# Linear attention on one core: the first v from two queues, another order of the first four heads, and v in two groups of eight tiles in every buffer

## The chip, the cores and the metric

The kernel runs on one core of a Trainium2 chip. TensorE (PE) multiplies, with its weight loads shown apart (PEld); VectorE (DVE), ScalarE (ACT) and GpSimd (POOL) do elementwise work; SyncE (SP) issues the DMA transfers, which 16 DMA engines carry out. The metric is the device time of one execution in microseconds, the median of several runs. It holds the profile's span, from the first to the last instruction, and a little around it.

## The reference

Inputs q, k and v and the output are bf16 arrays of 1 x 32 x 2048 x 128: 32 heads, 2048 positions, 128 columns.

```python
phi_q = jnp.where(q > 0, q + 1, jnp.exp(q)) + 1e-6
phi_k = jnp.where(k > 0, k + 1, jnp.exp(k)) + 1e-6
kv = jnp.einsum("bhsd,bhse->bhde", phi_k, v)
z = jnp.einsum("bhsd->bhd", phi_k)
num = jnp.einsum("bhqd,bhde->bhqe", phi_q, kv)
den = jnp.einsum("bhqd,bhd->bhq", phi_q, z)[..., None] + 1e-6
return num / den
```

## The kernel before

A head's 2048 positions lie on 128 partitions, 16 consecutive positions on each, so that a load or a store moves one run of 4,096 bytes per partition, and position tile j is the j-th position of every partition. The feature map is split as phi(x) = min(exp(x), 1) + 1e-6 + max(x, 0). The first part is called emk or emq, the second rk or rq, and most products are made twice, once with each, and added up in PSUM.

The steps of a head, with the names that the profile shows:

- ScalarE makes ek = exp(k) (line 276). VectorE makes emk of it (L282). GpSimd makes rk (L279; for head 1 VectorE does), and for tiles 1 to 5 it adds emk into rk (L287), which spares their second product.
- TensorE forms kv, summed over the 16 tiles, in one PSUM bank (L297 and L236). The sum z is formed beside it, as one more column. In SBUF, v lies between strips of ones (GAP, 32 columns). A tile at the edge of a group takes a column of ones in with its 128 columns of v, so its matmul has 129 columns. For every other tile a second matmul of one column follows with the weights still in place (`mm_held`, L236). The list `GROUPS` gives the number of groups of v in each of the six input buffers: one group of 16 tiles in buffers 0 to 3, two groups of 8 tiles in buffers 4 and 5. Head h uses buffer h mod 6. A load of v (L269) moves one run of 4,096 bytes per partition for one group, two of 2,048 for two.
- ScalarE copies kv to SBUF (kvs, L306), and VectorE adds the two columns of z to it (zs, L308).
- TensorE transposes the 16 tiles of q into xT (tr, L315). ScalarE makes eq = exp (L322) and the second half of rq (L330), VectorE the first half of rq (L326; all of it for heads 0 and 1) and emq (L333).
- TensorE multiplies both parts by kvs (num, L349 and L350), five PSUM banks to a head. VectorE adds 1e-6 to the denominators (den, L371), takes reciprocals (L377) and multiplies (L382, L389). SyncE stores the head (L434; the last one in two pieces of 288 and 224 KB).

`Plan` holds the order. Every step is added with an engine and a key; each engine runs its steps by rising key, in one queue, and waits on semaphores for what it reads or overwrites. A key is the head's number plus an offset of the step; the table `place` (L251) gives other keys to some steps of heads 0 to 3 and of the last head. On TensorE the order is tr(0), kv(0), tr(1), num(0), kv(1), tr(2), kv(2), num(1), tr(3), kv(3), num(2) and so on. SyncE's loads run ahead by up to six heads, as buffers come free; stores have keys that fall further behind from head to head (L438), with ten output buffers. Ahead of the first transposes, 42 matmuls on zeros (L242 to L247) run on TensorE, and GpSimd makes the identity and the ones (L227 to L234).

Of the kernel before, what the change touches and what calls it, by code (L numbers as in the profile page):

```python
# [11 lines left out]
def _ap(base: bass.AP, elem_offset: int, dims):  # L12
    return bass.AP(base.tensor, base.offset + elem_offset, [list(base.ap[0])] + [list(d) for d in dims])
# [131 lines left out]
def bass_standalone__linear_attn_elu__prompt_kernel(  # L145
# [6 lines left out]
    B, H, S, D = q.shape  # L152
    assert D == P and S == 16 * P
    NT = 16
# [3 lines left out]
    NBI = 6  # L158
    NBO = 10
# [3 lines left out]
    HALF = NT * P // 2  # L163
# [2 lines left out]
    ADD = (1, 2, 3, 4, 5)  # L166
    SPLIT = tuple(j for j in range(NT) if j not in ADD)
    GAP = 32
    GROUPS = (1, 1, 1, 1, 2, 2)
    VW = NT * D + 3 * GAP  # L170

    qf = q.rearrange("b h s d -> (b h) s d")
    kf = k.rearrange("b h s d -> (b h) s d")
# [3 lines left out]
    with ExitStack() as es:  # L177
        def sb(name, shape, dt):
            return es.enter_context(nc.sbuf_tensor(name, shape, dt))

        k_sb = sb("k_sb", [P, NBI, NT * D], bf16)
# [22 lines left out]
        def dma_sem(name):  # L204
            return dsems[name]

        for n, c in (("k", NBI), ("q", NBI), ("v", NBI), ("o", NBO + 1)):
            for i in range(c):
                dsems[(n, i)] = es.enter_context(nc.semaphore(f"s_{n}{i}"))

        block = es.enter_context(nc.Block())
        pl = Plan()

        def rows(x, h):
            return x[h].rearrange("(p j) d -> p (j d)", j=NT)

        vfull, ofull = v_sb[:, :, :], o_ps[:, :]
        xfull = xT_ps[:, :].bitcast(fp32)

        def vcol(bi, j):  # L220
            n = NT // GROUPS[bi]
            return GAP * (j // n + 1) + D * j, j % n == 0, j % n == n - 1

        zero_sb = o_sb[:, NBO - 1, 0, :]
# [3 lines left out]
        pl.add("pool", -8, lambda g: g.affine_select(out=ident[:], in_=ident[:], compare_op=ALU.not_equal, fill=1.0,  # L228
                                                     base=0, pattern=[[-1, P]], channel_multiplier=1),
               reads=[("id0",)], writes=[("ident",)])  # L230
        n1 = GROUPS.count(1)
        pl.add("pool", -7, lambda g: g.memset(_ap(vfull, 0, [[VW, n1], [GAP + NT * D, 2], [1, GAP]]), 1.0), writes=[("vones", 1)])
        pl.add("pool", -6.5, lambda g: g.memset(_ap(vfull, n1 * VW, [[VW, NBI - n1], [GAP + NT * D // 2, 3], [1, GAP]]), 1.0),
               writes=[("vones", 2)])  # L234
        def mm_held(pe, out_ap, rhs, stop):
            return pe.add_instruction(mybir.InstMatmult(  # L236
                start_tensor_calc=False, stop_tensor_calc=stop, ldweights=False, bass_skip_group_check=True,
                tile_position=(0, 0), tile_size=(P, P), name=nc.get_next_instruction_name(), engine=mybir.EngineType.PE,
                ins=[pe.lower_ap(rhs), pe.lower_ap(held[0])], outs=[pe.lower_ap(out_ap)]))

        held = [None]
        WARM = 42  # L242

        def warm(pe):
            for w in range(WARM):
                b = 2 + w % 3
                last = pe.matmul(o_ps[:, b * 512 + 3 * NC: b * 512 + 3 * NC + 125], lhsT=zero_sb, rhs=zero_sb[:, 0:125], start=True, stop=True)  # L247
            return last
        pl.add("pe", -9, warm, reads=[("warm",)], writes=[("banko", 2), ("banko", 3), ("banko", 4)])

        place = {("ek", 1): -1.05, ("ek", 2): -0.05, ("ek", 3): 1.02, ("kvs", 2): 1.01,  # L251
                 ("emk", 0): -2.05, ("rq", 0): -2.0, ("rk", 1): -1.95, ("emq", 0): -1.9, ("zs", 0): -1.75, ("emk", 1): -1.7,
                 ("rq", 1): 0.911, ("emk", 2): 0.921, ("zs", 1): 0.922, ("emq", 1): 0.923,
                 ("num", 0): -0.22,
                 ("zs", LAST): LAST - 1 + 0.902, ("kvs", LAST): LAST - 1 + 0.72}

        for h in range(NH):
            def at(name, key, h=h):
                return place.get((name, h), h + key)

            bi, b2, b3, bo = h % NBI, h % 2, h % 3, h % NBO

            def load(name, buf, src, key, h=h, bi=bi):
                dst, rws = buf[:, bi], rows(src, h)
                if name == "v":
                    n = GROUPS[bi]
                    dst = _ap(vfull, bi * VW + GAP, [[GAP + NT * D // n, n], [1, NT * D // n]])
                    rws = rws.rearrange("p (a b) -> p a b", a=n)
                pl.add("sp", key, lambda sp: sp.dma_start(dst, rws), writes=[(name, bi)], dma=(name, bi))  # L269

            load("k", k_sb, kf, h - NBI - (1.0 if h < 4 else 1.95))
            load("v", v_sb, vf, h - NBI - 0.8)
            load("q", q_sb, qf, h - NBI - 0.9)

            pl.add("act", at("ek", -2.8),
                   lambda a, bi=bi, b2=b2: a.activation(ek_sb[:, b2, :], k_sb[:, bi, :], ACT.Exp),  # L276
                   reads=[("k", bi)], writes=[("ek", b2)])
            pl.add("dve" if h == 1 else "pool", at("rk", 0),
                   lambda e, bi=bi, b3=b3: e.tensor_scalar(rk_sb[:, b3, :], k_sb[:, bi, :], BIG, 0.0, op0=ALU.min, op1=ALU.max),  # L279
                   reads=[("k", bi)], writes=[("rk", b3), ("rkx", b3), ("phik", b3)])  # L280
            pl.add("dve", at("emk", -3 + 0.95),
                   lambda d, b2=b2, b3=b3: d.tensor_scalar(emk_sb[:, b3, :], ek_sb[:, b2, :], 1.0, EPS, op0=ALU.min, op1=ALU.add),  # L282
                   reads=[("ek", b2)], writes=[("emk", b3)])

            def added(x, b3=b3):
# [3 lines left out]
                reads=[("emk", b3), ("rkx", b3)] + ([("emq", (h - 1) % 3)] if h else []), writes=[("phik", b3)])  # L289

            def kv(pe, tiles, srcs, bi=bi, b3=b3):
                for j in tiles:
                    for src in srcs:
                        first, fin = (j == SPLIT[0] and src is emk_sb), j == ADD[-1]
                        w = src[:, b3, j * D:(j + 1) * D]
                        c, l, r = vcol(bi, j)
                        last = pe.matmul(kvz_ps[:, 1 - l:NC + r], lhsT=w, rhs=v_sb[:, bi, c - l:c + D + r], start=first, stop=fin,  # L297
                                         skip_group_check=True)
                        if not l + r:
                            held[0] = w  # L300
                            last = mm_held(pe, kvz_ps[:, 0:1], ones_sb[:, 0:1], fin)
                return last
            pl.add("pe", at("kv", -1.2), lambda pe, kv=kv: kv(pe, SPLIT, (emk_sb, rk_sb)),
                   reads=[("emk", b3), ("rk", b3), ("v", bi), ("ones",), ("vones", GROUPS[bi])], writes=[("bankkv",)])
            pl.add("pe", at("kv", -1.2), lambda pe, kv=kv: kv(pe, ADD, (rk_sb,)), reads=[("phik", b3), ("v", bi)], writes=[("bankkv",)])
            pl.add("act", at("kvs", -0.95), lambda a, b3=b3: a.activation(kvs_sb[:, b3, 1:], kvz_ps[:, 1:NC], ACT.Copy),  # L306
                   reads=[("bankkv",)], writes=[("kvs", b3)])
            pl.add("dve", at("zs", -1 + 0.905), lambda d, b3=b3: d.tensor_scalar(  # L308
                kvs_sb[:, b3, 0:1], kvz_ps[:, 0:1], kvz_ps[:, NC:NC + 1], None, op0=ALU.add),
                   reads=[("bankkv",)], writes=[("zs", b3)])  # L310
# [8 lines left out]
            for half in (0, 1):  # L319
# [3 lines left out]
                   reads=both, writes=[("eq", b2)])  # L323
            cut = NT * P if h < 2 else HALF
            pl.add("dve", at("rq", -2 + 0.948),
                   lambda d, b3=b3, cut=cut: d.tensor_scalar(rq_sb[:, b3, :cut], xT_ps[:, :cut], 0.0, None, op0=ALU.max),  # L326
                   reads=both[:1 + (h < 2)], writes=[("rq", b3, 0)])
            if h > 1:
                pl.add("act", h - 1.0,
                       lambda a, b3=b3: a.activation(rq_sb[:, b3, HALF:], xT_ps[:, HALF:], ACT.Relu),  # L330
                       reads=[("bankx", 1)], writes=[("rq", b3, 1)])
            pl.add("dve", at("emq", -2 + 0.955),
                   lambda d, b2=b2, b3=b3: d.tensor_scalar(emq_sb[:, b3, :], eq_sb[:, b2, :], 1.0, EPS, op0=ALU.min, op1=ALU.add),  # L333
                   reads=[("eq", b2)], writes=[("emq", b3)])
# [139 lines left out]
```

## Time and profile before

| | us |
|---|---|
| median of 3 runs | 170.79 (170.34 to 171.24) |
| the profiled execution: device time | 170.33 |
| its span, first to last instruction | 168.5 |
| busy: PE / PEld / DVE / ACT / POOL | 159.2 / 156.6 / 151.3 / 155.7 / 103.6 |
| DMA: bytes moved, mean rate | 67.53 MB, 401 GB/s |
| median from issue to landing, loads of k / q / v, stores | 14.3 / 14.1 / 14.2 / 14.7 |

The profile page gives each engine's busy time and its share of the span, the share of each DMA queue, and the chain of work that ended last. A row of instructions gives line, engine, operation, output and inputs with their shapes, the count, and what the engine waited for just before. In a table of stages each engine's busy time is followed by its number of instructions; the last three columns are the granted TensorE clock, the mean share of the 16 DMA engines that was busy, and GB/s. The DMA view gives the time from the issue of a transfer to its last landing; cut to a window, it tells it for the transfers issued in that window. A transfer counts as landed when the last of the 16 engines has delivered its part.

### The profile page before, as it was taken

The page shows a single profiled execution, that of the slowest core. Times are in us where ns is not written, and L with a number is a line of the kernel's source. Part 1 is how long each engine was busy: PE and PEld are TensorE (multiplying, and loading weights), DVE is VectorE, ACT ScalarE, POOL GpSimd, SP SyncE. Part 2 cuts the span into 40 slices and gives each one's busy share as a digit, 9 for nine tenths or more (in the row PEclk, how much of TensorE's full clock was granted, in tenths as well). Part 3 has the DMA queues.
Part 4 walks back from the last instruction along what each step waited for, and adds up shares of the span by engine and source line. Part 5 has one row for each costly group of instructions (what it writes and reads, how often), then busy time and mean ns, then how long its engine had stood idle before and what let it go on. Part 6 is the DMA issues. An engine that isn't in the chain of part 4 may idle for free.

```text
span 168.5 us, 6557 instructions
## 1 busy us (share of the span) xinstructions
PE 159.2 (94%) x3202; PEld 156.6 (93%) x2506; DVE 151.3 (90%) x295; ACT 155.7 (92%) x142; POOL 103.6 (61%) x71
## 2 busy tenths in 40 slices
PE   7699979999999999999999999999999999999980
PEld 7589969999999999999999999999999999999970
DVE  0177689999999999999999999999999999999973
ACT  3877999999999999999999999999999999999682
POOL 2706756666677766666777666667776666667300
PEclk9999999999999999999999999999999999999996
DMA  5999999999999999999999999999999999999966
GB/s 191 382 420 413 419 408 415 412 407 423 409 413 412 415 421 410 414 417 409 418 415 413 419 414 415 408 414 420 414 417 416 415 415 413 417 418 412 397 276 269
DMA packets 19884, 67.53 MB, mean 401 GB/s; under 512 B 2064, under 2 KB 2192, under 8 KB 19856
## 3 DMA queue, kind: packets, MB, share of 16 engines
q1 hardware_dynamic: 19856, 67.12, 99.0%
q8 instruction: 22, 0.36, 0.8%
q14 instruction: 6, 0.05, 0.1%
HBM read 50.33 MB, written 16.78 MB: 398 GB/s over the span
## 4 chain that ended last, share of the span: by engine, by line
PE 86%; DMA 4%; ACT 4%; DVE 3%; SPq 1%; issue 0%; DVEq 0%
PE kvz_ps L297 35%; PE o_ps L349 17%; PE o_ps L350 17%; PE xT_ps L315 15%; DMA k_sb<-in_k_dram 4%; ACT ek_sb L276 2%; DVE o_sb L389 1%; PE kvz_ps L236 1%; ACT eq_sb L322 1%; SPq L269 1%; ACT rq_sb L330 1%; DVE emk_sb L282 0%; DVE emq_sb L333 0%; DVE den_sb L371 0%; DVE rden_sb L377 0%
## 5 line engine op out<-in xcount | busy, mean ns | idle before, releaser
L287 POOL TENSOR_TENSOR rk_sb<-rk_sb,emk_sb 128x640 bf16<-128x640 bf16 x32 | 44.7, 1398 | 51.4 <-DVE emq_sb L333 41.3
L297 PE MATMUL kvz_ps<-v_sb,rk_sb 128*128 128x128 bf16 (+1 forms) x512 | 69.3, 218 | 0.2 <-POOL rk_sb L287 0.2
L389 DVE TENSOR_TENSOR o_sb<-o_ps,rden_sb 128x768 bf16<-128x768 f32 (+2 forms) x62 | 67.8, 1134 | 0.0
L322 ACT ACTIVATE eq_sb<-xT_ps 128x2048 bf16<-128x2048 bf16 x32 | 60.1, 1877 | 4.5 <-PE xT_ps L315 3.4
L276 ACT ACTIVATE ek_sb<-k_sb 128x2048 bf16<-128x2048 bf16 x32 | 61.4, 1922 | 2.9 <-DMA k_sb<-in_k_dram 2.9
L349 PE MATMUL o_ps<-kvs_sb,emq_sb 128*128 128x129 bf16 (+1 forms) x536 | 61.1, 217 | 0.4 <-DVE o_sb L382 0.2
L350 PE MATMUL o_ps<-kvs_sb,rq_sb 128*128 128x129 bf16 (+1 forms) x536 | 61.1, 217 | 0.0
L279 POOL TENSOR_SCALAR rk_sb<-k_sb 128x2048 bf16<-128x2048 bf16 x31 | 58.8, 1895 | 2.3 <-DMA k_sb<-in_k_dram 2.3
L236 PE MATMUL kvz_ps<-ones_sb,rk_sb 128*128 128x1 bf16 x428 | 59.6, 165 | 0.0
L297 PE MATMUL kvz_ps<-v_sb,emk_sb 128*128 128x128 bf16 (+1 forms) x352 | 56.8, 218 | 2.7 <-DMA v_sb<-in_v_dram 1.4
L349 PEld LDWEIGHTS o_ps<-kvs_sb,emq_sb 128*128 128x128 bf16 x536 | 50.5, 98 | 0.8 <-DVE o_sb L382 0.4
L350 PEld LDWEIGHTS o_ps<-kvs_sb,rq_sb 128*128 128x128 bf16 x536 | 50.1, 97 | 0.0
L297 PEld LDWEIGHTS kvz_ps<-v_sb,rk_sb 128*128 128x128 bf16 x512 | 46.7, 96 | 1.4 <-POOL rk_sb L287 0.3
L236 PE MATMUL kvz_ps<-ones_sb,emk_sb 128*128 128x1 bf16 x268 | 44.0, 165 | 0.0
L297 PEld LDWEIGHTS kvz_ps<-v_sb,emk_sb 128*128 128x128 bf16 x352 | 33.8, 96 | 3.0 <-DMA v_sb<-in_v_dram 1.6
L315 PE MATMUL xT_ps<-ident,q_sb 128*128 128x128 bf16 x512 | 33.8, 219 | 0.3 <-DMA q_sb<-in_q_dram 0.3
L330 ACT ACTIVATE rq_sb<-xT_ps 128x1024 bf16<-128x1024 bf16 x30 | 30.5, 1018 | 0.0
L315 PEld LDWEIGHTS xT_ps<-ident,q_sb 128*128 128x128 bf16 x512 | 29.9, 98 | 0.7 <-DMA q_sb<-in_q_dram 0.7
L282 DVE TENSOR_SCALAR emk_sb<-ek_sb 128x2048 bf16<-128x2048 bf16 x32 | 21.9, 684 | 6.9 <-ACT ek_sb L276 6.9
L326 DVE TENSOR_SCALAR rq_sb<-xT_ps 128x1024 bf16<-128x1024 bf16 (+1 forms) x32 | 23.1, 721 | 1.6 <-ACT eq_sb L322 1.6
L333 DVE TENSOR_SCALAR emq_sb<-eq_sb 128x2048 bf16<-128x2048 bf16 x32 | 21.9, 685 | 0.0
L382 DVE TENSOR_TENSOR o_sb<-o_ps,rden_sb 128x128 bf16<-128x128 f32 x31 | 9.0, 290 | 1.0
(26 smaller groups left out, 51.7 us busy)
## 6 DMA issues: line engine op xcount, KB each, us to landing
k_sb<-in_k_dram SPq DMA_DIRECT2D x32, 512.0 KB, 14.3
q_sb<-in_q_dram SPq DMA_DIRECT2D x32, 512.0 KB, 14.1
v_sb<-in_v_dram SPq DMA_DIRECT2D x32, 512.0 KB, 14.2
out_dram<-o_sb SPq DMA_DIRECT2D x31, 512.0 KB, 14.7
out_dram<-o_sb SPq DMA_DIRECT2D x1, 288.0 KB, 2.5
out_dram<-o_sb SPq DMA_DIRECT2D x1, 224.0 KB, 2.4
```

Of the source, the lines that this page charges most:

```text
L236: return pe.add_instruction(mybir.InstMatmult(start_tensor_calc=False, stop_tensor_calc=stop, ldweights=False, bass_skip_group_check=True, ...
L276: lambda a, bi=bi, b2=b2: a.activation(ek_sb[:, b2, :], k_sb[:, bi, :], ACT.Exp),
L279: lambda e, bi=bi, b3=b3: e.tensor_scalar(rk_sb[:, b3, :], k_sb[:, bi, :], BIG, 0.0, op0=ALU.min, op1=ALU.max),
L287: pl.add("pool", h + 0.5, lambda g, added=added: g.tensor_tensor(out=added(rk_sb), in0=added(rk_sb), in1=added(emk_sb), op=ALU.add), reads ...
L297: last = pe.matmul(kvz_ps[:, 1 - l:NC + r], lhsT=w, rhs=v_sb[:, bi, c - l:c + D + r], start=first, stop=fin, skip_group_check=True)
L315: last = pe.transpose(xT_ps[:, j * P:(j + 1) * P], q_sb[:, bi, j * P:(j + 1) * P], ident[:])
L322: pl.add("act", h - 1.1, lambda a, b2=b2: a.activation(eq_sb[:, b2, :], xT_ps[:, :], ACT.Exp), reads=both, writes=[("eq", b2)])
L326: lambda d, b3=b3, cut=cut: d.tensor_scalar(rq_sb[:, b3, :cut], xT_ps[:, :cut], 0.0, None, op0=ALU.max),
L330: lambda a, b3=b3: a.activation(rq_sb[:, b3, HALF:], xT_ps[:, HALF:], ACT.Relu),
L349: pe.matmul(o_ap, lhsT=emq_sb[:, b3, t * P:(t + 1) * P], rhs=kvs_sb[:, b3, c0:c1], start=True, stop=False)
L350: return pe.matmul(o_ap, lhsT=rq_sb[:, b3, t * P:(t + 1) * P], rhs=kvs_sb[:, b3, c0:c1], start=False, stop=True)
L389: pl.add("dve", key, lambda d: d.tensor_tensor(out=o_sb[:, bo, 3 * g0:3 * g1, :].rearrange("p (a b) d -> p a b d", b=3), in0=_ap(full, bas ...
```

## The change

All six buffers hold v in two groups of 8 tiles, so every load of v has two runs of 2,048 bytes per partition, and 19 held matmuls are left in every head instead of 23 in the one-group heads. The ones are written by one memset in place of two. The first v is loaded in two transfers: partitions 0 to 15 are issued from ScalarE's queue ahead of all its other work, with a semaphore of their own, the other 112 from SyncE's as before; kv(0) waits for both. In SyncE's order, the load of head 3's k stands ahead of that of head 2's v instead of behind it. On VectorE rk(1) and emq(0) stand ahead of rq(0); emk(3) moves ahead of head 0's last products, and zs(2) right behind them. On ScalarE ek(3) stands ahead of eq(2) and rq(2) instead of behind them and kvs(2). There are 41 matmuls on zeros instead of 42.

```diff
--- before.py
+++ after.py
@@ -166,7 +166,7 @@
     ADD = (1, 2, 3, 4, 5)
     SPLIT = tuple(j for j in range(NT) if j not in ADD)
     GAP = 32
-    GROUPS = (1, 1, 1, 1, 2, 2)
+    NV = 2
     VW = NT * D + 3 * GAP
 
     qf = q.rearrange("b h s d -> (b h) s d")
@@ -204,7 +204,7 @@
         def dma_sem(name):
             return dsems[name]
 
-        for n, c in (("k", NBI), ("q", NBI), ("v", NBI), ("o", NBO + 1)):
+        for n, c in (("k", NBI), ("q", NBI), ("v", NBI), ("va", 1), ("o", NBO + 1)):
             for i in range(c):
                 dsems[(n, i)] = es.enter_context(nc.semaphore(f"s_{n}{i}"))
 
@@ -218,7 +218,7 @@
         xfull = xT_ps[:, :].bitcast(fp32)
 
         def vcol(bi, j):
-            n = NT // GROUPS[bi]
+            n = NT // NV
             return GAP * (j // n + 1) + D * j, j % n == 0, j % n == n - 1
 
         zero_sb = o_sb[:, NBO - 1, 0, :]
@@ -228,10 +228,7 @@
         pl.add("pool", -8, lambda g: g.affine_select(out=ident[:], in_=ident[:], compare_op=ALU.not_equal, fill=1.0,
                                                      base=0, pattern=[[-1, P]], channel_multiplier=1),
                reads=[("id0",)], writes=[("ident",)])
-        n1 = GROUPS.count(1)
-        pl.add("pool", -7, lambda g: g.memset(_ap(vfull, 0, [[VW, n1], [GAP + NT * D, 2], [1, GAP]]), 1.0), writes=[("vones", 1)])
-        pl.add("pool", -6.5, lambda g: g.memset(_ap(vfull, n1 * VW, [[VW, NBI - n1], [GAP + NT * D // 2, 3], [1, GAP]]), 1.0),
-               writes=[("vones", 2)])
+        pl.add("pool", -7, lambda g: g.memset(_ap(vfull, 0, [[VW, NBI], [GAP + HALF, 3], [1, GAP]]), 1.0), writes=[("vones",)])
         def mm_held(pe, out_ap, rhs, stop):
             return pe.add_instruction(mybir.InstMatmult(
                 start_tensor_calc=False, stop_tensor_calc=stop, ldweights=False, bass_skip_group_check=True,
@@ -239,7 +236,7 @@
                 ins=[pe.lower_ap(rhs), pe.lower_ap(held[0])], outs=[pe.lower_ap(out_ap)]))
 
         held = [None]
-        WARM = 42
+        WARM = 41
 
         def warm(pe):
             for w in range(WARM):
@@ -248,9 +245,10 @@
             return last
         pl.add("pe", -9, warm, reads=[("warm",)], writes=[("banko", 2), ("banko", 3), ("banko", 4)])
 
-        place = {("ek", 1): -1.05, ("ek", 2): -0.05, ("ek", 3): 1.02, ("kvs", 2): 1.01,
-                 ("emk", 0): -2.05, ("rq", 0): -2.0, ("rk", 1): -1.95, ("emq", 0): -1.9, ("zs", 0): -1.75, ("emk", 1): -1.7,
-                 ("rq", 1): 0.911, ("emk", 2): 0.921, ("zs", 1): 0.922, ("emq", 1): 0.923,
+        place = {("ek", 1): -1.05, ("ek", 2): -0.05, ("ek", 3): 0.1,
+                 ("emk", 0): -2.05, ("rk", 1): -2.0, ("emq", 0): -1.95, ("rq", 0): -1.9, ("zs", 0): -1.75, ("emk", 1): -1.7,
+                 ("rq", 1): 0.911, ("emk", 2): 0.921, ("zs", 1): 0.922, ("emq", 1): 0.923, ("emk", 3): 0.924,
+                 ("zs", 2): 0.9455,
                  ("num", 0): -0.22,
                  ("zs", LAST): LAST - 1 + 0.902, ("kvs", LAST): LAST - 1 + 0.72}
 
@@ -263,12 +261,16 @@
             def load(name, buf, src, key, h=h, bi=bi):
                 dst, rws = buf[:, bi], rows(src, h)
                 if name == "v":
-                    n = GROUPS[bi]
+                    n = NV
                     dst = _ap(vfull, bi * VW + GAP, [[GAP + NT * D // n, n], [1, NT * D // n]])
                     rws = rws.rearrange("p (a b) -> p a b", a=n)
-                pl.add("sp", key, lambda sp: sp.dma_start(dst, rws), writes=[(name, bi)], dma=(name, bi))
-
-            load("k", k_sb, kf, h - NBI - (1.0 if h < 4 else 1.95))
+                p0 = 0
+                if name == "v" and h == 0:
+                    p0 = 16
+                    pl.add("act", -20, lambda a: a.dma_start(dst[0:p0], rws[0:p0]), writes=[("va", 0)], dma=("va", 0))
+                pl.add("sp", key, lambda sp: sp.dma_start(dst[p0:], rws[p0:]), writes=[(name, bi)], dma=(name, bi))
+
+            load("k", k_sb, kf, h - NBI - (1.0 if h < 3 else 1.85 if h == 3 else 1.95))
             load("v", v_sb, vf, h - NBI - 0.8)
             load("q", q_sb, qf, h - NBI - 0.9)
 
@@ -301,7 +303,7 @@
                             last = mm_held(pe, kvz_ps[:, 0:1], ones_sb[:, 0:1], fin)
                 return last
             pl.add("pe", at("kv", -1.2), lambda pe, kv=kv: kv(pe, SPLIT, (emk_sb, rk_sb)),
-                   reads=[("emk", b3), ("rk", b3), ("v", bi), ("ones",), ("vones", GROUPS[bi])], writes=[("bankkv",)])
+                   reads=[("emk", b3), ("rk", b3), ("v", bi), ("ones",), ("vones",)] + ([("va", 0)] if h == 0 else []), writes=[("bankkv",)])
             pl.add("pe", at("kv", -1.2), lambda pe, kv=kv: kv(pe, ADD, (rk_sb,)), reads=[("phik", b3), ("v", bi)], writes=[("bankkv",)])
             pl.add("act", at("kvs", -0.95), lambda a, b3=b3: a.activation(kvs_sb[:, b3, 1:], kvz_ps[:, 1:NC], ACT.Copy),
                    reads=[("bankkv",)], writes=[("kvs", b3)])
```

## The prediction, made before the change was run

> **What bounds the kernel now.** I read the page first, then the chain of waits, then the DMA view cut to single issues.
>
> ```profile
> PE 159.2 (94%) x3202; PEld 156.6 (93%) x2506; DVE 151.3 (90%) x295; ACT 155.7 (92%) x142; POOL 103.6 (61%) x71
> ...
> q1 hardware_dynamic: 19856, 67.12, 99.0%
> ...
> PE 86%; DMA 4%; ACT 4%; DVE 3%; SPq 1%; issue 0%; DVEq 0%
> ```
>
> The chain names TensorE, but the one queue of loads and stores is busy for 99.0% of the span. Two paths have to be followed to the end.
>
> The path of the engines first. In the chain, the transposes of heads 5, 6, 7 and 8 begin at:
>
> ```profile
> 31.87 0.89 PE xT_ps L315 x16
> ...
> 36.61 0.89 PE xT_ps L315 x16
> ...
> 41.43 0.89 PE xT_ps L315 x16
> ...
> 46.26 0.89 PE xT_ps L315 x16
> ```
>
> Head 5 has its v in two groups and takes 4.74 us; heads 6 and 7, in one group, take 4.82 and 4.83. Nothing interrupts TensorE there. On the timeline ScalarE's Exp of q starts at 28.07 and 32.80 around the two-group head 4: 4.73 us without idle time, so ScalarE is next in line. VectorE's sums of the denominators start at 27.34 and 31.99: 4.65 us.
>
> Now the path of the transfers. The last five stores are issued at 154.72, 159.54, 163.69, 165.02 and 165.68 us. The DMA view, cut to each issue, gives the time to its last landing:
>
> ```profile
> out_dram<-o_sb SPq DMA_DIRECT2D x1, 512.0 KB, 9.6
> ...
> out_dram<-o_sb SPq DMA_DIRECT2D x1, 512.0 KB, 6.0
> ...
> out_dram<-o_sb SPq DMA_DIRECT2D x1, 512.0 KB, 3.1
> ...
> out_dram<-o_sb SPq DMA_DIRECT2D x1, 288.0 KB, 2.5
> ...
> out_dram<-o_sb SPq DMA_DIRECT2D x1, 224.0 KB, 2.4
> ```
>
> They land at 164.3, 165.5, 166.8, 167.5 and 168.1: steps of 1.2 and 1.3 us for 512 KB, 0.7 for 288 KB, 0.6 for 224 KB. Those are the steps of the whole run (28 stores land on average 1.261 us after the transfer before them). So the slowest of the 16 DMA engines has no gap up to the last byte, although the stores were issued up to 4.8 us apart. The stages show how few engines that is:
>
> ```profile
> 156.00:158.00 2.00, 2.00 (x43) 1.99 (x33) 1.92 (x6) 0.54 (x1) 1.40 (x1) 1.00 1.02 414
> ...
> 163.00:164.00 1.00, 0.73 (x12) 0.55 (x10) 0.41 (x3) 1.00 (x6) 0.00 (x0) 1.00 0.50 201
> ```
>
> At 163 us half of the 16 engines are idle, waiting for the next store; the others still have a backlog. The mean share hides that. The last store is issued right after VectorE's last product, so both paths end together: **a faster TensorE alone cannot end the kernel earlier.**
>
> **The change, part by part.**
>
> *Held one-column matmuls.* Two groups make tiles 7 and 8 edge tiles, two sources each: 4 fewer at L236 per one-group head, 88 in the 22 heads of buffers 0 to 3. The chain prices four at 4.82 - 4.73 = 0.09 us. That is 18 x 0.09 = 1.6 us for heads 6 on and 0.4 for heads 0 to 3: 2.0 us off the engines' path. ScalarE's 4.73 then meets TensorE's 4.73, so no more is to be had.
>
> *v in 2 KB halves.* The same 22 loads become 256 packets instead of 128. Buffers 4 and 5 already do this. I read every landing as above: ten two-group loads of v land 1.299 us after the transfer before them, 18 one-group loads 1.271. The difference, 0.028, times 22 is 0.62 us more for each DMA engine, and it is all on the transfers' path. Bounds: from below nothing, since the bytes are the same and no row shows a gain; from above the two-group step against that of k, 1.299 - 1.223 = 0.076, or 1.67 us. I take 0.62, the row of the same tensor. The Trainium skill (DMA: Bandwidth & Descriptors, Specifications) gives 512 B as the smallest transfer at line rate, by which 2 KB halves would cost nothing and the sum would be 0.62 lower; the ten loads speak against it.
>
> *16 partitions of the first v from ScalarE's queue.* The first four transfers are issued at 0.73, 1.18, 1.65 and 2.11, and their times to landing are
>
> ```profile
> k_sb<-in_k_dram SPq DMA_DIRECT2D x1, 512.0 KB, 3.4
> ...
> q_sb<-in_q_dram SPq DMA_DIRECT2D x1, 512.0 KB, 4.2
> ...
> v_sb<-in_v_dram SPq DMA_DIRECT2D x1, 512.0 KB, 6.2
> ...
> k_sb<-in_k_dram SPq DMA_DIRECT2D x1, 512.0 KB, 7.0
> ```
>
> so they land at 4.1, 5.4, 7.9 and 9.1. The first v holds 2.5 us, 1.25 more than its neighbours, and work waits for both:
>
> ```profile
> 7.92 0.23 PE L297 MATMUL kvz_ps<-v_sb,emk_sb 128*128 128x129 bf16 x1 [1.45 <-DMA v_sb<-in_v_dram]
> ...
> 9.17 1.91 ACT L276 ACTIVATE ek_sb<-k_sb 128x2048 bf16<-128x2048 bf16 x1 [0.79 <-DMA k_sb<-in_k_dram]
> ```
>
> If the loss belongs to the first touch of v, an early touch from another queue hides it. How much of it does the engine that ends last get back? Not all: the landing of the second q (head 2) steps 1.8 us, with a 16 KB instruction packet on the queue just before; the same kind of packet makes steps of 2.6 at head 16's k. Had the engine late at the first v been hit again, that step too would have been 2.6. So the last one is another, at most 2.6 - 1.8, taken from 1.25, = 0.4 us late at the first v. Bounds 0 and 0.4; I take 0.2. The Trainium skill (same page, Issuing engines are not separate DMA queues) says that DMAs of all issuers interleave on the same 16 engines and only issue time is saved; by that the 0.2 is nothing and the sum 0.2 higher. No run here shows a second queue. ScalarE's issue (0.4 us, as SP's) stands ahead of its table load (0.74 to 2.02) and the Exp at 4.14: 1.7 us of cover. The 64 KB may push the first k back by an eighth of 1.25, 0.16 us, or fit ahead of it; that reorders bytes and adds none.
>
> *Order of the first heads.* On VectorE rk(1) moves ahead of rq(0) and waits for the second k; emq(0), rq(0), zs(0) and tr(1), which needs xT free, queue behind it. If k still lands at 9.15, rk ends at 9.8, emq at 10.4, rq at 11.6: tr(1) starts at 11.6 instead of 10.43. ScalarE makes ek(3) before eq(2), in the gaps of 0.55 and 0.64 us before kvs(1) and eq(2); emk(3) and zs(2) no longer stand behind ek(3)'s wait of 1.8 us, which ends TensorE's stall of 1.2 before head 3's kv. k(3) is loaded before v(2), so v(2) lands a step later, 17.2, about when kv(2) can start (17.0). Followed through, tr(4) starts at 26.7 against 26.98: 0.3 us gained with the first v as late as now, about 1.5 without. One warm matmul less (4.29 / 42 = 0.1 us) and one memset for two end before 5.4, when q(0) lands; kv's wait for the sixteen partitions is over long before 7.9.
>
> **Sum.** Engines' path: -2.0 and -0.3 to -1.5. Transfers' path: +0.62 - 0.2 = +0.4. The later one decides. Profiled execution: span 168.5, 1.8 around it, 170.33 in all, so 170.75. The three runs have a median of 170.79, 0.46 above the profiled one; delays of the engines, which reach the end now, would lie under 2 us of cover, other delays would not. I put the **predicted time at 170.9**.
>
> What is late next: loads. v(28) lands at 140.5 and is used at 142.97. Its use comes 20 x 0.09 = 1.8 us and the gain at the start sooner, its landing 20 x 0.028 = 0.6 later: 2.4 of cover is gone by head 28 and TensorE begins to wait there, up to about 1 us. That costs nothing, since the engines then still end over a microsecond early.
>
> **Rivals.**
>
> *The engines alone set the end* (faster): the steps at the end would be a coincidence of issue times, and the stores would follow the engines. 170.33 - 2.0 - 0.3 = 168.0. For it: the chain. Against it: the even steps of stores issued unevenly.
>
> *Halves are dear* (slower): place, the engine that lands last; price 0.076 a load, +1.67, and no gain at the first v: 172.0. It decides from (0.85 + 0.2) / 22 = 0.048 a load on. For it: v steps by more than k in both forms, so short or oddly placed runs do cost. Against it: the ten loads measured.
>
> *Halves cost nothing*: 170.33 - 0.2 = 170.1. That is what the skill's 512 B would make of it.
>
> *The early touch does nothing*: the first v still steps 2.5; 170.95, inside the forecast.
>
> **Chances.** Transfers set the end with halves at about 0.03: 0.58, its own range 170.3 to 171.6. Engines alone: 0.13. Dear halves: 0.20. Free halves: 0.09. A measurement of this kernel tells about 0.5%, 0.85 us, from no change. Faster by more: 0.13 and 0.02 from the edges of the other cases. Slower by more: most of the dear halves, 0.18, and 0.06 from the forecast's upper edge. The rest, 0.61, is within. The range, 169.5 to 172.0, takes in both ends of the halves and leaves out the engines alone and a little above.
>
> **What would show it.** Right: stores at the end issued over a microsecond earlier than now, landing still in steps of 1.25 until the last; heads of 4.73 throughout until waits for k, q or v appear after head 25; v's steps near 1.30 in every buffer; the first v landing near 6.7. Wrong: last stores landing with gaps between them and the span shorter by 2 us or more (engines alone); steps of v at 1.32 or more; a start whose tr(4) comes later than 27.

## The result, and the profile after

The changed kernel takes 171.83 us, the median of 11 runs (171.38 to 172.47), beside 170.72 for 11 runs of the kernel before on the same chip (170.34 to 171.24). The ratio is 1.0064, with a 95% interval of 1.0049 to 1.008: 1.1 us slower, where the forecast was 170.9. The profiled execution took 171.51, its span is 169.6, 1.1 more than before.

The page after, with the lines that answer to the three of before (busy time of the engines; packets, MB and share of the load and store queue; the chain by engine):

```profile
PE 156.8 (92%) x3113; PEld 154.0 (91%) x2505; DVE 151.5 (89%) x295; ACT 155.1 (91%) x142; POOL 104.1 (61%) x70
...
q1 hardware_dynamic: 22640, 67.05, 99.4%
...
PE 85%; DVE 5%; DMA 4%; ACT 1%; SPq 1%; issue 0%; DVEq 0%
```

TensorE does 2.4 us less work and the kernel is slower. The queue has 2,784 packets more (22 loads x 128, less the 32 that no longer go through it) and is busy for 99.4% of a longer span.

The chain after, from the transposes of head 3 on (start, duration):

```profile
23.33 0.89 PE xT_ps L317 x16
...
28.06 0.89 PE xT_ps L317 x16
...
32.78 0.89 PE xT_ps L317 x16
...
37.53 0.89 PE xT_ps L317 x16
...
42.25 0.89 PE xT_ps L317 x16
```

Every head now takes 4.72 to 4.75 us; one-group heads took 4.82. So the held matmuls are gone at the price that was read. But head 3's transposes begin over 2 us later than before (23.17 against 20.77 on TensorE's timeline), head 4's 0.9 later (27.89 against 26.98).

The last five stores after, from the DMA view cut to each issue; they are issued at 154.09, 158.81, 162.88, 164.19 and 164.86:

```profile
out_dram<-o_sb SPq DMA_DIRECT2D x1, 512.0 KB, 11.3
...
out_dram<-o_sb SPq DMA_DIRECT2D x1, 512.0 KB, 7.8
...
out_dram<-o_sb SPq DMA_DIRECT2D x1, 512.0 KB, 5.0
...
out_dram<-o_sb SPq DMA_DIRECT2D x1, 288.0 KB, 4.4
...
out_dram<-o_sb SPq DMA_DIRECT2D x1, 224.0 KB, 4.3
```

They land at 165.4, 166.6, 167.9, 168.6 and 169.2, in the same even steps as before. The last store is issued 0.8 us earlier than before and lands 1.1 later: the time to landing grew from 2.4 to 4.3 us. The engines got through earlier, and the transfers set the end.

The stages after (engines' busy time, then granted clock, DMA share, GB/s):

```profile
163.00:164.00 1.00, 0.00 (x0) 0.00 (x0) 0.97 (x3) 1.00 (x6) 0.00 (x0) 1.00 0.77 315
165.00:166.00 1.00, 0.00 (x0) 0.00 (x0) 0.00 (x0) 0.00 (x0) 0.00 (x0) 0.50 1.03 412
```

TensorE is through by 163 us. From 165 on nothing runs but the transfers, at their full rate.

### The profile page after: what moved, and what is told of

Its sections match the earlier page's. It is cut to its first block, busy times and chain, and to the rows that moved or that the text cites. A ratio compares the mean times of both kernels' runs of the same rounds, so it can differ in the third digit from the quotient of the medians.

```text
span 169.6 us, 6468 instructions
## 1 busy us (share of the span) xinstructions
PE 156.8 (92%) x3113; PEld 154.0 (91%) x2505; DVE 151.5 (89%) x295; ACT 155.1 (91%) x142; POOL 104.1 (61%) x70
## 3 DMA queue, kind: packets, MB, share of 16 engines
q1 hardware_dynamic: 22640, 67.05, 99.4%
## 4 chain that ended last, share of the span: by engine, by line
PE 85%; DVE 5%; DMA 4%; ACT 1%; SPq 1%; issue 0%; DVEq 0%
PE kvz_ps L299 34%; PE o_ps L351 17%; PE o_ps L352 17%; PE xT_ps L317 16%; DMA k_sb<-in_k_dram 4%; DVE o_sb L391 3%; ACT ek_sb L278 1%; PE kvz_ps L233 1%; SPq L271 1%; DVE emk_sb L284 1%; DVE rq_sb L328 1%; DVE rk_sb L281 0%; DVE emq_sb L335 0%; DVE rden_sb L379 0%; DVE den_sb L373 0%
## 5 line engine op out<-in xcount | busy, mean ns | idle before, releaser
L391 DVE TENSOR_TENSOR o_sb<-o_ps,rden_sb 128x768 bf16<-128x768 f32 (+2 forms) x62 | 67.8, 1134 | 0.0
L299 PE MATMUL kvz_ps<-v_sb,rk_sb 128*128 128x128 bf16 (+1 forms) x512 | 67.0, 218 | 0.0
L299 PE MATMUL kvz_ps<-v_sb,emk_sb 128*128 128x128 bf16 (+1 forms) x352 | 54.7, 218 | 0.4 <-DMA v_sb<-in_v_dram 0.3
L233 PE MATMUL kvz_ps<-ones_sb,rk_sb 128*128 128x1 bf16 x384 | 52.5, 165 | 0.0
L233 PE MATMUL kvz_ps<-ones_sb,emk_sb 128*128 128x1 bf16 x224 | 36.9, 166 | 0.0
L284 DVE TENSOR_SCALAR emk_sb<-ek_sb 128x2048 bf16<-128x2048 bf16 x32 | 22.4, 701 | 6.4 <-ACT ek_sb L278 6.3
```

The lines of the kernel that those rows point to most:

```text
L233: return pe.add_instruction(mybir.InstMatmult(start_tensor_calc=False, stop_tensor_calc=stop, ldweights=False, bass_skip_group_check=True, ...
L391: pl.add("dve", key, lambda d: d.tensor_tensor(out=o_sb[:, bo, 3 * g0:3 * g1, :].rearrange("p (a b) d -> p a b d", b=3), in0=_ap(full, bas ...
```

## The experiments

Each kernel stands beside runs of the kernel before on the same chip, and the ratio is to those. It comes from several rounds, and can differ slightly from that of the two medians. The question of the first four: which part costs the 1.1 us?

**before_nv2**: the kernel before with two groups in every buffer, with one memset for the ones, and nothing else.

```diff
-    GROUPS = (1, 1, 1, 1, 2, 2)
+    GROUPS = (2, 2, 2, 2, 2, 2)
-        n1 = GROUPS.count(1)
...
-        pl.add("pool", -6.5, lambda g: g.memset(_ap(vfull, n1 * VW, [[VW, NBI - n1], [GAP + NT * D // 2, 3], [1, GAP]]), 1.0),
...
+        pl.add("pool", -7, lambda g: g.memset(_ap(vfull, 0, [[VW, NBI], [GAP + NT * D // 2, 3], [1, GAP]]), 1.0), writes=[("vones", 2)])
```

> The kernel before with v in two groups in all six buffers and nothing else. Theory, the transfers set the end and their loss of 1.1 us has two parts (0.6 from 22 loads of v in halves, 0.5 from the first v on a second queue): +0.6 us, 171.3; the last stores are issued about 2 us earlier than before and still land in steps of 1.25 until the end. Rival A, all 1.1 us come from the halves (0.05 a load): +1.1 us, 171.8. Rival B, the engines set the end: -2.0 us, 168.7.

Measured: 171.72 beside 170.80, ratio 1.0053 (1.0033 to 1.0073). Its last stores are issued at 153.63, 158.36, 162.43, 163.74 and 164.40; the times to landing of the first and of the last two:

```profile
out_dram<-o_sb SPq DMA_DIRECT2D x1, 512.0 KB, 12.0
...
out_dram<-o_sb SPq DMA_DIRECT2D x1, 288.0 KB, 5.1
out_dram<-o_sb SPq DMA_DIRECT2D x1, 224.0 KB, 5.0
```

The engines end 1.3 us earlier than before and the last byte lands 1.3 later, at 169.4. The halves alone make up 0.92 of the 1.1 us, with an interval of 0.56 to 1.25. That is 0.042 us for each of the 22 loads, where 0.028 was predicted.

**before_va**: the kernel before with 16 partitions of the first v from ScalarE's queue.

```diff
+                p0 = 0
+                if name == "v" and h == 0:
+                    p0 = 16
+                    pl.add("act", -20, lambda a: a.dma_start(dst[0:p0], rws[0:p0]), writes=[("va", 0)], dma=("va", 0))
-                pl.add("sp", key, lambda sp: sp.dma_start(dst, rws), writes=[(name, bi)], dma=(name, bi))
+                pl.add("sp", key, lambda sp: sp.dma_start(dst[p0:], rws[p0:]), writes=[(name, bi)], dma=(name, bi))
```

> The kernel before with 16 partitions of the first v from ScalarE's queue and nothing else. Theory of the two parts: +0.5 us, 171.2, with the loss visible in the landings of the first k and q (k at 4.5 and q at 6.6 instead of 4.1 and 5.4). Rival A, all from the halves: 170.7, no change. Engines and transfers end together in the kernel before, so a start of the engines that comes later by x adds x, whatever the transfers do.

Measured: 170.63 beside 170.80, ratio 0.9995 (0.9982 to 1.0007). The first k lands 0.4 us later (4.48), the first v 0.5 earlier (7.38), the second k 0.6 earlier (8.54), and the last store at 168.17 instead of 168.05. So this part is worth nothing either way: the predicted gain of 0.2 is not there, and neither is the loss of half a microsecond that I suspected after the result.

**before_order**: the kernel before with the new order alone: `place`, the load of head 3's k ahead of head 2's v, and 41 matmuls on zeros.

```diff
-        WARM = 42
+        WARM = 41
-        place = {("ek", 1): -1.05, ("ek", 2): -0.05, ("ek", 3): 1.02, ("kvs", 2): 1.01,
-                 ("emk", 0): -2.05, ("rq", 0): -2.0, ("rk", 1): -1.95, ("emq", 0): -1.9, ("zs", 0): -1.75, ("emk", 1): -1.7,
+        place = {("ek", 1): -1.05, ("ek", 2): -0.05, ("ek", 3): 0.1,
+                 ("emk", 0): -2.05, ("rk", 1): -2.0, ("emq", 0): -1.95, ("rq", 0): -1.9, ("zs", 0): -1.75, ("emk", 1): -1.7,
...
-            load("k", k_sb, kf, h - NBI - (1.0 if h < 4 else 1.95))
+            load("k", k_sb, kf, h - NBI - (1.0 if h < 3 else 1.85 if h == 3 else 1.95))
```

> The kernel before with the order of the first four heads of the kernel after (the table of places, head 3's k loaded ahead of head 2's v, 41 matmuls on zeros). Theory: the transfers are the same in number and form, so they end at the same time; the engines start by -0.3 us (worked out before) to +0.9 us (measured in the kernel after) and end by as much later: 170.7 to 171.6. Transposes of head 4 at about 26.7 if the late start in the kernel after came from the second queue, at about 27.9 if it came from the order.

Measured: 171.08 beside 170.80, ratio 1.0015 (0.9995 to 1.0034), which can't be told from no change. The profile can tell more. Head 4's transposes start at 27.92, as in the changed kernel, so the late start belongs to the order and not to the second queue. The last stores are issued at 164.62, 165.97 and 166.63, 0.95 us later than before; the times of the last three:

```profile
out_dram<-o_sb SPq DMA_DIRECT2D x1, 512.0 KB, 2.7
...
out_dram<-o_sb SPq DMA_DIRECT2D x1, 288.0 KB, 2.2
...
out_dram<-o_sb SPq DMA_DIRECT2D x1, 224.0 KB, 2.1
```

They land at 167.3, 168.2 and 168.7: 0.9 after one another for 288 KB where a backlog gave 0.7. In this profile there is no backlog left for these stores and the engines set the end, some 0.6 us later than in the profile before; the medians differ by 0.3. In the changed kernel the faster heads hide this.

**after_no_va**: the changed kernel with the first v in one transfer from SyncE.

```diff
-                if name == "v" and h == 0:
-                    p0 = 16
-                    pl.add("act", -20, lambda a: a.dma_start(dst[0:p0], rws[0:p0]), writes=[("va", 0)], dma=("va", 0))
```

> The kernel after with the whole first v from SyncE's queue. Theory of the two parts: 0.5 us less than the kernel after, 171.3; q lands at 5.4 again and the first v at 7.9. Rival A, all from the halves: 171.8, as the kernel after. The engines are under cover here, so their start does not matter.

Measured: 171.71 beside 170.80, ratio 1.0052 (1.0034 to 1.007), the same as the changed kernel's within the intervals. The theory that the second queue is half of the loss has fallen from both sides.

The next question was whether the transfers really set the end, or only seem to.

**before_light**: the kernel before, with less work for TensorE and the transfers as they were. The one-column matmuls of tiles 7 and 8 are left out in the one-group heads, so z lacks these tiles.

```diff
-                        if not l + r:
+                        if not (l + r or j in (7, 8)):
```

> The kernel before, with TensorE's work of the kernel after and the transfers of the kernel before: the held one-column matmuls of tiles 7 and 8 are left out in the one-group heads, so z lacks these tiles there. Theory, the slowest DMA engine sets the end: at most -0.3 us (170.5), with the last store issued 1.5 to 2 us earlier and landing as late as before. Rival, the engines set the end: -2.0 us, 168.8.

Measured: 170.55 beside 170.66, ratio 1.0001 (0.9986 to 1.0016). The last stores are issued 2.2 us earlier than before, at 152.71, 157.43, 161.51, 162.81 and 163.47, with these times to landing:

```profile
out_dram<-o_sb SPq DMA_DIRECT2D x1, 288.0 KB, 5.0
out_dram<-o_sb SPq DMA_DIRECT2D x1, 224.0 KB, 4.9
```

The last byte lands at 168.4 (168.1 before). This decides it: the very saving on TensorE that the change makes, without the halves that pay for it, is worth nothing (at most 0.3 us by the interval). It turns into waiting for the DMA engines.

**after_less**: the changed kernel with one store fewer.

```diff
+            if h == 20:
+                pass
-            if h < LAST:
+            elif h < LAST:
```

> The kernel after with one transfer fewer: the store of head 20 is left out, so that head of the output is not written. Theory, the transfers set the end: 1.25 us come off the transfers' path, of which the engines' path, which ends 0.8 us earlier than in the kernel before, lets 0.8 to 1.2 through: 170.6 to 171.0. Rival, the engines set the end: 171.8, as the kernel after.

Measured: 170.94 beside 170.66, ratio 1.0015 (0.9999 to 1.0032). It is the only one of these edits that takes transfers away, and the changed kernel gets 0.8 us back by the ratios, 0.9 by the medians, where a full step of a store is 1.27. The last store still needs 3.5 us to land. So time at the end follows the bytes; whether one for one, this measurement can't tell.

**all_one**: the kernel before with one group in every buffer: the opposite of the change.

```diff
-    GROUPS = (1, 1, 1, 1, 2, 2)
+    GROUPS = (1, 1, 1, 1, 1, 1)
```

> The kernel before with v in one group in all six buffers: ten loads lose their halves and ten heads get four held matmuls more. Theory, both paths end together in the kernel before: the transfers end 0.3 to 0.4 us earlier, the engines 10 x 0.09 = 0.9 us later and set the end: 171.7. Rival, only the transfers count: 170.4. The last stores should land with gaps between them, by their issue times.

Measured: 171.07 beside 170.66, ratio 1.0022 (1.0008 to 1.0036). The last store is issued at 166.58, 0.9 us later than before, and lands after 2.1 us at 168.6. With the held matmuls back in ten more heads the engines set the end. The forecast of 171.7 had let all of the 0.9 through. The loss, 0.4 us, is smaller, because before a part of that time went to waiting for the backlog: the last store needs 2.1 us to land instead of 2.4. That explains 0.3 of the missing 0.5.

**three_two** and **first_two**: two groups in one more buffer, the fourth or the first, to see how the price of the halves grows.

```diff
-    GROUPS = (1, 1, 1, 1, 2, 2)
+    GROUPS = (1, 1, 1, 2, 2, 2)
```

```diff
-    GROUPS = (1, 1, 1, 1, 2, 2)
+    GROUPS = (2, 1, 1, 1, 2, 2)
...
```

In first_two the ones are written by three memsets, by buffers, in place of two.

> The kernel before with buffer 3 in two groups as well, five loads in halves more (heads 3, 9, 15, 21, 27). Theory, a load in halves costs the transfers about 0.03 us once the queue is full, and the rest of the 0.9 us for 22 loads is lost at the start, with the first loads of v: +0.15 us, 170.85; the engines end 0.45 us earlier, under cover. Rival, every load costs the same, 0.04: +0.2 us. The two differ by less than the interval; what counts is the kernel with buffer 0.

> The kernel before with buffer 0 in two groups as well, six loads in halves more (heads 0, 6, 12, 18, 24, 30), the first v among them. Theory, the first load of v in halves loses 0.35 to 0.5 us by itself: +0.5 to +0.65 us, 171.3, and between 4 and 8 us of the span the queue moves 320 GB/s, as in the kernel with two groups everywhere, and not 375. Rival, every load costs the same, 0.04: +0.25 us, 170.95, and 375 GB/s there.

Measured: 170.80 and 170.72 beside 170.49, ratios 1.0015 (0.9998 to 1.0032) and 1.0013 (0.9997 to 1.0029). These are 5 and 6 more halved loads at 0.05 and 0.04 us each, if anything; the intervals take in nothing too. The first load of all, when halved alone, does not cost the half microsecond that I had put on it. So the list of the kernel before is a flat optimum: from all_one to three_two the medians lie within 0.4 us of it (all_one's interval lies just above no change), and only two groups everywhere is worse by more.

**nv2_gap128**: before_nv2 with strips of ones of 128 columns instead of 32, so that each half starts at another place in SBUF.

```diff
-    GAP = 32
+    GAP = 128
...
```

> The kernel before with two groups in all six buffers and strips of 128 ones instead of 32, so that every run of v in SBUF begins on a multiple of 256 bytes, where it began 64, 128 or 192 bytes off or on one. Theory, a load in halves is dear because of its two packets: 171.7, as with strips of 32, and v's landings still step by 1.30. Rival, it is dear because of where its runs begin: steps of v near 1.24, the transfers about 1.5 us shorter, and 170.2 or less, below both kernels.

Measured: 173.07 beside 170.66, ratio 1.0148 (1.0125 to 1.0171), 1.35 us over before_nv2 by the medians, 1.6 by the ratios. The middle step of v (the median from head 6 on) stays at 1.29 us, that of q grows from 1.237 to 1.253. Both theories missed: the place of the halves is not what makes them dear, and why wider strips cost this much stays open.

**nv2_low8**: before_nv2 with the stores of heads 20 to 28 cut into 112, 8 and 8 partitions.

```diff
+            if h in range(20, 29):
+                cuts = (0, 112) + tuple(range(112 + 8, P + 1, 8))
+                for i, (p0, p1) in enumerate(zip(cuts, cuts[1:])):
+                    pl.add("sp", late + 0.001 * i, lambda sp, h=h, bo=bo, p0=p0, p1=p1: sp.dma_start(
+                        rows(of, h)[p0:p1], o_sb[p0:p1, bo].rearrange("p j d -> p (j d)")),
+                        reads=[("o", bo, p) for p in ("t", 0, 1, 2, 3, 4)], dma=("o", bo))
```

> Two groups in all six buffers in the order of the kernel before (171.72), and the stores of heads 20 to 28 each cut into one of 112 partitions and two of 8, which eight of the 16 DMA engines carry. Theory, the end is set by the backlog of those engines that the instruction packets have delayed, eight of 16 by the busy share at 163 us: if the eight that take the small stores are others, each of nine stores spares the late ones one packet of 0.156 us, 1.4 in all: 170.4, and the engines, which end 1.3 us earlier than before, let it through. If they are the same eight: +1.4 us, 173.1. Rival, the backlog is the same on all 16: 171.7.

Measured: 173.38 beside 170.49, ratio 1.018 (1.0154 to 1.0205), 1.66 us over before_nv2. That is near the case in which the small stores go to the very engines that are late, but the trace offers another cause. From 150.7 to 161.8 us SyncE's issues take 1.0 to 1.7 us each, where those from 143.4 to 149.8 took 0.3 to 0.9. The store of head 29 is issued at 163.78 instead of 158.36 in before_nv2, the last one at 165.83 instead of 164.40, although VectorE's last product starts 0.6 us earlier. The rate falls meanwhile:

```profile
155.00:160.00 5.00, 5.00 (x105) 4.95 (x84) 4.71 (x13) 3.61 (x6) 1.33 (x1) 1.00 0.94 338
160.00:165.00 5.00, 1.67 (x25) 1.21 (x22) 3.18 (x10) 3.33 (x13) 0.00 (x0) 0.95 0.90 283
```

So late issues have a share in the loss, and this run doesn't tell which engines the small stores went to. The Trainium skill (DMA: Bandwidth & Descriptors, Why a DMA increments its semaphore by 16 and not by 1) says that a transfer of SyncE whose partitions spread over only k engines takes the lowest-numbered k of the 16. By that all the small stores would meet the same eight engines; no run here shows it.

**before_few**: the kernel before with about 2,060 of TensorE's some 5,700 instructions left out, for what else makes some DMA engines late.

```diff
-            pl.add("pe", at("kv", -1.2), lambda pe, kv=kv: kv(pe, SPLIT, (emk_sb, rk_sb)),
+            pl.add("pe", at("kv", -1.2), lambda pe, kv=kv: kv(pe, SPLIT, (emk_sb,)),
-                    pe.matmul(o_ap, lhsT=emq_sb[:, b3, t * P:(t + 1) * P], rhs=kvs_sb[:, b3, c0:c1], start=True, stop=False)
-                    return pe.matmul(o_ap, lhsT=rq_sb[:, b3, t * P:(t + 1) * P], rhs=kvs_sb[:, b3, c0:c1],
-                                     start=False, stop=True)
+                    return pe.matmul(o_ap, lhsT=emq_sb[:, b3, t * P:(t + 1) * P], rhs=kvs_sb[:, b3, c0:c1], start=True, stop=True)
```

> The kernel before with some 2,060 of TensorE's 5,700 instructions left out: the products with rk of the eleven tiles that are not added (with their held matmuls) and all products with rq, so the output lacks those parts. The transfers of q, k, v and the output are the same. Theory, the late DMA engines are late by the 16 KB instruction packets, of which the latest take three in turn (at 12, 70 and 125 us, 1.3 to 1.4 us each): about 14 packets are left instead of 22, two at most for one engine, and the last store lands 1.3 us earlier: 169.3. Rival, the steps of 2.6 us at heads 16 and 27 have another cause that comes with time or bytes: 170.5, since faster engines alone changed nothing.

Measured: 168.91 beside 170.59, ratio 0.9918 (0.9901 to 0.9936). The page of before_few has 14 instruction packets, where that of before and after have 22:

```profile
q8 instruction: 14, 0.23, 0.5%
```

The line before and after the change:

```profile
q8 instruction: 22, 0.36, 0.8%
```

Its last stores are issued at 151.10, 155.76, 159.82, 160.59 and 161.37, with these times to landing for the last three:

```profile
out_dram<-o_sb SPq DMA_DIRECT2D x1, 512.0 KB, 5.5
...
out_dram<-o_sb SPq DMA_DIRECT2D x1, 288.0 KB, 5.4
out_dram<-o_sb SPq DMA_DIRECT2D x1, 224.0 KB, 5.2
```

They land at 165.3, 166.0 and 166.6. The same loads and stores end 1.5 us earlier than before. A faster TensorE was worth nothing in before_light, so what helps here is, by all that these runs show, the smaller program. In the kernel before, the landing steps grow where an instruction packet lies on the queue: 1.8, 2.6 and 2.6 us beside packets at 12.3, 70.0 and 125.3 us, eight packets apart each time. So a packet of 16 KB makes one engine some 1.3 us late (2.6 less a usual step of 1.26). In the changed kernel, too, the large steps (2.4, 2.7 and 2.7 us) stand beside the first, ninth and seventeenth packet; in before_few 1.8 and 2.4 beside the first and ninth. The even distance suggests that the packets take turns over eight engines; then, with eight fewer, each of those is hit once less.

The trace also tells when each of the 16 engines delivered its part of a transfer, by the updates of its semaphore. The first of them delivers its part of head 28's store at 159.52 us in the kernel before and at 159.48 in before_few, so the transfers as such went no faster. But the latest seven follow 4.2 to 4.8 us behind the first in the one and 3.0 to 3.4 behind in the other. In before_nv2 already the first engine is 0.7 us later than before, at 160.26: the halves cost even the engine that is least behind, the instruction packets only some. The DMA engines are not equally loaded, and this is why the last one has no gap while half of the others are idle.

The Trainium skill (Runtime: NRT & Kernel Launch, Instruction fetch mechanics) says that an engine's instructions are refilled in blocks of 16 KiB and that crossing a block is mostly hidden. The first agrees with the page of before (22 packets, 0.36 MB). The second does not hold where the data transfers are the bound: there, 14 instead of 22 go with 1.7 us.

## Why the prediction was right, and where it was off

The mechanism of the forecast came true, but 171.83 lies above its own range of 170.3 to 171.6. It is inside the stated range only because that was drawn up to 172.0 for the rival of dear halves.

**Both paths end together, and the transfers decide.** Shown. The engines ended 0.8 us earlier in the changed kernel, 1.3 in before_nv2 and 2.2 in before_light, and the time rose or stayed. The rival in which the engines alone set the end would have made before_light about 168.8; it is out. The other side of the same statement also holds: in before_order and all_one the engines came later, and in their profiles they set the end.

**Held matmuls, 0.09 us a head.** Right: 4.72 to 4.75 us in all heads. From head 4's transposes to the last store the changed kernel gained 1.7 us against a predicted 1.6. At the end it was worth nothing, as predicted.

**Halves, 0.62 us in all.** This is the term that was mis-sized: before_nv2 measures 0.92. Its interval alone (0.56 to 1.25) still takes in 0.62; that of the changed kernel (0.84 to 1.37), whose other parts came to nothing at the end, does not.

A part of the miss is the reading. The views round the time to landing to a tenth, and the ten and 18 loads read through them gave 1.299 and 1.271. Read from the trace without rounding, they land 1.290 and 1.258 us after the transfer before them: 0.032 a load and 0.70 in all. In the changed kernel the 18 loads of the first four buffers, from head 6 on, step by 1.290 too (1.258 before), and those of the last two buffers by 1.304. The Trainium skill (DMA: Bandwidth & Descriptors, Why small descriptors are slow) has about 3 cycles of overhead for each packet. By an estimate from that, with beats of 32 B, two halves need 134 cycles for 131, 2.3% of a step of 1.26 us or 0.03 us: the steps agree.

The remainder, some 0.2 us, may be lost early, as far as single profiles tell. Here are the windows from 4 to 8 us, in which only the first loads move, of the kernel before,

```profile
4.00:8.00 4.00, 2.46 (x34) 2.12 (x32) 0.69 (x1) 3.41 (x2) 2.96 (x2) 1.00 1.01 375
```

of before_nv2,

```profile
4.00:8.00 4.00, 2.01 (x32) 1.66 (x29) 0.69 (x1) 3.38 (x2) 3.04 (x2) 1.00 0.92 319
```

and of the changed kernel:

```profile
4.00:8.00 4.00, 2.24 (x34) 1.90 (x31) 0.70 (x1) 2.11 (x2) 2.58 (x2) 1.00 1.01 343
```

The rate falls from 375 to 319 and 343 GB/s. These rates scatter: before_light, before_order and before_few, whose first loads are those of the kernel before, have 406, 360 and 346. But all six profiles with halves everywhere lie below that, at 271 to 343. If so, the step failed in what it took the early loads to be: the row came from loads of buffers 4 and 5, all of which land after the start. first_two, with only the first load halved, has 362 GB/s there, which is no less than the scatter of whole loads. Which of the early loads lose the time, and why, stays open. 0.042 us a load stays under the 0.048 from which the rival of dear halves was to decide, and yet its sign came true: 1.1 us is just over the 0.85 that this measurement can tell from no change.

**First v from two queues, -0.2.** Measured as nothing (0.9995). In the profile after, the stall is no longer at the first v but at q. The first issues after, in the DMA view (issued at 0.74, 1.18, 1.64 and 2.37 us):

```profile
v_sb<-in_v_dram ACTq DMA_DIRECT2D x1, 64.0 KB, 4.1
...
q_sb<-in_q_dram SPq DMA_DIRECT2D x1, 512.0 KB, 5.5
...
v_sb<-in_v_dram SPq DMA_DIRECT2D x1, 448.0 KB, 6.1
...
k_sb<-in_k_dram SPq DMA_DIRECT2D x1, 512.0 KB, 6.7
```

The first k lands at 4.5, q at 6.7, v at 7.8 and the second k at 9.0. Now it is q that steps by 2.2 us and v by 1.1; all four are through about where they were. The second queue need not be the cause: in before_light, which has none, the first v steps by 1.4 us and lands at 6.8, and in before_va none of the first four loads of SyncE steps by more than 1.6. So the stall that this term was to hide does not come in every execution, and its 1.25 us, read in one profile, are no fixed price. The rule of the Trainium skill that the prediction weighed (DMA: Bandwidth & Descriptors, Issuing engines are not separate DMA queues) gives nothing for this term, and the ratio agrees with it. The first v was predicted at 6.7 if its stall was hidden; it landed at 7.8, as now.

**Order of the first heads, 0.3 us gained at the start.** Wrong, with the opposite sign: 0.9 us lost at head 4, past the 27 that the prediction had named as a sign of being wrong. The first part was followed rightly, tr(1) at 11.6 predicted and 11.69 found. Later emk(3) falls on GpSimd's rk, and both are slow. VectorE's timeline after:

```profile
18.70 1.25 DVE L284 TENSOR_SCALAR emk_sb<-ek_sb 128x2048 bf16<-128x2048 bf16 x1 [0.79 <-ACT ek_sb L278]
19.86 2.21 DVE L391 TENSOR_TENSOR o_sb<-o_ps,rden_sb 128x768 bf16<-128x768 f32 x2
22.00 0.21 DVE L310 TENSOR_SCALAR kvs_sb<-kvz_ps 128x1 bf16<-128x1 f32 x1
22.13 0.68 DVE L328 TENSOR_SCALAR rq_sb<-xT_ps 128x1024 bf16<-128x1024 bf16 x1
```

GpSimd's:

```profile
19.36 2.34 POOL L281 TENSOR_SCALAR rk_sb<-k_sb 128x2048 bf16<-128x2048 bf16 x1
```

and TensorE's:

```profile
22.13 0.23 PE L351 MATMUL o_ps<-kvs_sb,emq_sb 128*128 128x129 bf16 x1 [0.28 <-DVE o_sb L391]
...
23.17 1.06 PE L317 MATMUL xT_ps<-ident,q_sb 128*128 128x128 bf16 x16
```

emk(3) takes 1.25 us, where the mean of its kind is 0.70, and GpSimd's rk 2.34, where its mean is 1.91. Head 0's last products (L391) stand behind emk(3) now and end at 22.0. TensorE's products of head 1 wait for them twice (0.86 and 0.28 us), and tr(3), next on TensorE, starts at 23.17 where 20.77 was the time before. My sum had taken each instruction at its usual duration. The 0.55 us that emk(3) takes longer are about half of the 1.2 by which tr(4) missed the 26.7 of the prediction; the rest isn't separated. It cost nothing here because two microseconds of cover lay over the engines; before_order shows the engines ending 0.95 later without that cover.

**Late next: waits for loads.** Not seen. The smallest distance between a load of v landing and its use shrank to 0.74 us, at head 28, and TensorE never waited. The engines came 0.9 us later than before, where 0.3 earlier was predicted, which left that much more room.

**The sum.** Halves 0.92 and not 0.62, first v 0 and not -0.2: 0.9 over the runs of the kernel before gives 171.6. The measured 171.83 is 0.2 above that, less than the uncertainty of one ratio (some 0.3 us), and no run separates it.

## What to carry to other kernels

Before a faster engine is credited, look at the time from issue to landing of the last stores: where they are issued unevenly and land in even steps, the latest DMA engine is the bound, whatever the chain of waits names, and engine time that is saved only lengthens that wait. Splitting a load into shorter runs is then paid on the path that matters, in every load, and the price has to be read separately for the start and for the steady part. When an order is followed through by hand, look for instructions of VectorE and GpSimd that will newly run at the same time, and don't count on their usual durations there.

## What the runs showed of the hardware

- An instruction packet of 16 KB holds one DMA engine up for some 1.3 us, and where the queue is never empty this stays on that engine until the end (the latest seven of 16 engines were 4.2 to 4.8 us behind the first at head 28's store). 14 packets instead of 22 went with 1.7 us less, the largest gain in any run here. The number of instructions of a program can be a cost in transfers.
- The stall of about 1.2 us at the first loads belongs to no tensor for certain: in the changed kernel the first q took it (a step of 2.2 us) in place of the first v (2.5), and in before_light and before_va it was missing.
- VectorE's emk and GpSimd's rk slow each other down where they overlap: 1.25 us and 2.34 where 0.70 and 1.91 are usual, with 0.59 us of overlap. This isn't so for all pairs: VectorE's products out of PSUM (L389) overlap GpSimd's work in nearly every head and keep their duration.
- Strips of ones of 128 columns instead of 32 cost 1.35 us. The rates are lower early (404 and 406 GB/s from 10 to 30 and from 30 to 50 us, where before_nv2 has 413 and 411) and nearly equal from 50 on (411 to 413 in both). The cause stays open.
